# Row tiles 4 and 5 of layer 2 without quarter folding in the inverse transform along d, in a kernel of two GFNet and two squared-ReLU layers

## The chip, the cores and the metric

The kernel runs on one core of one Trainium2 chip. The metric is device time in microseconds of that core, lower is better; the time before is a median of three runs. A profiled execution also shows the engines' work: PE (TensorE, matrix multiply; its weight loads are shown as PEld), DVE (VectorE), ACT (ScalarE), POOL (GpSimd) and SP, which here only issues DMAs.

## The reference, cut to what matters

```
def _A_ref(x, w_r, w_i):                      # x: 1 x 2048 x 448, bfloat16
    X = rfft2(x.astype(float32), axes=(-2, -1))
    X = X * (w_r + 1j * w_i)                  # w: 2048 x 225
    return irfft2(X, s=(S, D)).astype(bfloat16)

def _B_ref(x, w1, b1, w2, b2):                # w1: 448 x 1792
    h = relu(x @ w1 + b1)
    return (h * h) @ w2 + b2

x = A_x
for layer in range(2):
    x = x + _A_ref(layernorm(x), A_w_r, A_w_i)
    x = x + _B_ref(layernorm(x), B_w1, B_b1, B_w2, B_b2)
```

Each of the two layers filters all 2048 rows together in the frequency domain (a transform along the rows, s, and one along the 448 columns, d), and then runs a feed-forward network (FFN) on each row by itself.

## The kernel before, in words

Everything between the input and the output stays on chip. The 2048 rows are 16 row tiles of 128 (row 16 p + t is in tile t, partition p). The transforms are matmuls with constant matrices. Per layer the stages are:

- forward transform, per row tile in part A (A1, A2), then per pair p of low row frequencies: along d (TD), along the remaining row digit (B), the product with the weights on DVE (W), and the inverse of that digit (Bi). Their results go through `VT`, and every row tile needs all pairs.
- inverse along d per group of row tiles, `stage_TI` (line 1087), and the last inverse digit with the residual addition, `stage_AI` (line 1109). Groups are tile 0, tile 1, then pairs (2, 3), (4, 5) up to (14, 15). The layer norm statistics of the FFN (`ln_B`, line 1164) follow per group: a sum of squares (lines 1170 and 1171, on ACT or DVE), a square root (line 700, ACT), a reciprocal, and the transposed row tile `yT`, by `flip` (line 1151: matmuls with a reversed identity and a copy out of PSUM) for tiles 0 and 1, and by a transposing DMA (line 668, on SP) for the others; tiles 4 to 15 are scaled first (lines 717 and 718).
- FFN in four chunks of four row tiles. Chunk 0 has two groups of first-layer matmuls, for tiles 0 and 1 and for tiles 2 and 3 (`h_part`, line 1266, widths of 256); chunks 1 to 3 pair half-height matmuls of width 512 (`h_pairs`, line 1226). ACT does the ReLU out of PSUM (line 700), DVE squares it (line 735). `o_tile` (line 1280) is the second matrix product of one tile, 14 matmuls, and its addition to the residual (line 1292). In layer 2 each row tile then goes to memory.

**The two ways through the inverse along d.** A transform matrix along 448 columns has mirror symmetry: the right half of the cosine part is the mirror image of the left half, that of the sine part too, with a sign. Both ways use this (half folding: only 224 columns come out of `stage_TI`). Quarter folding uses it once more, on even and odd frequencies apart. With `late` true, `stage_TI` makes four separate products of 112 columns per tile, `stage_AI` adds and subtracts them on DVE by four `tt` (line 735, two from `tmp` to `VT`, two back) and then needs two matmuls of 224 columns per tile. With `late` false, `stage_TI` sums pairs of matmuls of 224 columns in PSUM, there is no `tt`, and `stage_AI` has four matmuls of 448 columns for a group of two tiles. Either way `stage_TI` has eight matmuls for a group of two, `stage_AI` four, ACT copies 2 x 448 columns out of PSUM (line 706), and DVE has two residual additions (line 1146).

`late` is `t >= LATE[L]`: with `LATE = (4, 4)` tiles 4 to 15 of both layers are quarter folded.

**The order of the work.** The program first lists all operations, grouped into units (a PSUM tile's matmuls, or one operation of another engine). A unit's number is its place in that list. `ORDER` fixes, for each engine, the sequence of unit numbers. The class `_Sched` then gives out PSUM banks in that order, sets the semaphore waits, and, by its own model of the times, puts filler matmuls on a constant (line 1415) where it sees PE idle. For copies out of PSUM that both ACT and DVE can do (`evac`, lines 706 and 707), the engine whose list holds the unit does them. Engines run their lists strictly in order.

Units that the text uses, with the numbers of before: layer 1: TI of tile 1 is 287 and 289 with copies 288 and 290, of tile 0 270 and 272 with copies 271 and 273; copies of TI of tiles 4/5 319, 6/7 337, 10/11 375, 12/13 393 (matmuls 392), 2/3 305, 14/15 411; folding sums 320 to 323 (tiles 4/5), 376 and 377 (tiles 10/11); square roots of tiles 0 and 1 277 and 294; first FFN matmuls 428. Layer 2: copy of the last tile's A2 858; Bi 944 and 946 with copies 945 and 947; copy of Bi 953; TI of tile 0 961 and 963 with copies 962 and 964, of tile 1 978 and 980 with copies 979 and 981; flip of tile 0 969 with copy 970, of tile 1 986 with copy 987; square roots 968 and 985; copies of TI of tiles 2/3 996, 4/5 1011, 6/7 1029, 8/9 1049, 10/11 1067, 12/13 1085; tiles 4/5: TI 1010, the four `tt` 1012 to 1015, AI 1016, residual additions 1017 and 1018; scaling of tile 7 1042; squares of tiles 10/11 1075 and 1076; TI of tiles 14/15 1102; first FFN matmuls 1120.

Of the kernel before, what the change touches and what calls it, by code (L numbers as in the profile page):

```python
# [36 lines left out]
def make_constants():  # L37
# [76 lines left out]
ADJ = {}  # L114
ORDER = {
    "pe": """
# [10 lines left out]
1354""",  # L127
    "act": """
# [12 lines left out]
1315 1325 1323 1330 1328 1335 1333 1338 1340""",  # L141
    "dve": """
# [23 lines left out]
1331 1329 1101 1334 1336 1339 1341 1119 1346 1349 1343 1352 1355""",  # L166
    "pool": """
12 15 13 16 17 14 18 20 19 22 21 53 69 61 23 77 24 85 25 116 119 26 142 145 129 132 158 155""",
    "sp": """
3 6 4 8 10 28 30 29 36 32 40 41 39 31 27 34 45 37 33 47 46 38 44 35 314 269 334 352 354 355 372 390 408 426 1005 1026  # L170
1044 1046 1064 1082 1047 1100 1118 1250 1209 1306 1303 1203 1212 1253 1259 1300 1297 1350 1206 1347 1256 1344 1353
1356""",
}
STAY = 3000.0
LOOK = {}
# [3 lines left out]
A1GROUPS = ((0, 1), (1, 1), (2, 1), (3, 1), (4, 1), (5, 1), (6, 2), (8, 2), (10, 2), (12, 2), (14, 2))  # L179
ACT_STATS = (1, 3, 5)  # L180
HALVES = True
LATE = (4, 4)


class _Op:
# [395 lines left out]
def bass_interleave_layers__spectral_gfnet__dense_activation_squared_relu__prompt_kernel(nc, A_x, A_w_r, A_w_i, B_x, B_w1, B_b1, B_w2, B_b2, out):  # L581
# [6 lines left out]
    with ExitStack() as es:  # L588
# [758 lines left out]
        def ffn(last):  # L1347
# [4 lines left out]
            for t, n in TGROUPS:  # L1352
                base = PR["ramp"][L] - PR["rstep"][L] * t if t < 4 else PR["late"][L] - PR["lstep"][L] * t
                sch.bias, sch.tag = base + PR["TI"][L], f"TI{L}.{t}"
                stage_TI(t, n, t >= LATE[L])
                sch.bias, sch.tag = base + PR["AI"][L], f"AI{L}.{t}"
                stage_AI(t, n, not last, t >= LATE[L])
                sch.bias, sch.tag = base, f"ln{L}.{t}"
# [135 lines left out]
```

## Time and profile before

| what | value |
|---|---|
| median of 3 runs | 267.29 us (266.42 to 267.77) |
| profiled execution, its own time | 267.07 us |
| its span, first to last instruction | 265.1 us |
| busy PE, DVE, ACT | 257.7, 204.1, 172.8 us |
| layer 1: inverse along d begins, first FFN matmul | 42.7, 50.3 us |
| layer 2: inverse along d begins, first FFN matmul | 166.8, 173.0 us |

Times in the profile are us from the first instruction, and each instruction carries the line of the helper that made it: nearly all matmuls are L681, copies out of PSUM L706 on ACT and L707 on DVE, sums and products of two tensors L735. Matmuls are pipelined, so that the length of one holds its latency, and the pace of a row of them is read from several. A row of the timeline merges neighbours of one kind: start, length from the first start to the last end, engine, line, operation, output<-inputs, shape, count, and in brackets the idle time ahead of it with what ended it. `TIo`, what `stage_TI` leaves, and the quarter folded sums lie in the buffers `tmp` and `VT` and appear under these names; `W1_sb` and `W2_sb` both appear as `W_sb`.

### The profile page before, as it was taken

Reading aid. Unit: us, or ns where it says so; the run is one execution under the profiler, and the core shown is the slowest. Engines: PE = TensorE matmul, PEld = TensorE weight load, DVE = VectorE, ACT = ScalarE, POOL = GpSimd, SP = SyncE. Lnnn points to the kernel's source line nnn. Section 1 sums busy time; section 2 is a strip of 40 time slices with the busy share of each in tenths; the row PEclk is TensorE's granted clock in tenths of the full one; section 3 lists DMA queues with packets and bytes.
Section 4 is the critical chain, followed back from the end, with each engine's and each line's share of the span. In section 5 each row is a group of like instructions: output and inputs, shape, how many; then the busy total and the mean of one; then the engine's idle time right before and its main releaser. Section 6 shows DMA issues by size and latency. Waiting matters only on the chain.

```text
span 265.1 us, 5674 instructions
## 1 busy us (share of the span) xinstructions
PE 257.7 (97%) x2127; PEld 163.0 (61%) x2127; DVE 204.1 (77%) x658; ACT 172.8 (65%) x375; POOL 14.3 (5%) x32
## 2 busy tenths in 40 slices
PE   8999989999999999999999999999999999999996
PEld 2686768797544555665558756789654465554454
DVE  3878998999969983489998899899964069921662
ACT  5887897999449447893216889999634886121820
POOL 8840000000000000000000000000000000000000
PEclk9999999999999999999999999999999999999999
DMA  7999700032300224000000000022232000220053
GB/s 226 383 262 350 262 3 2 0 72 41 74 2 1 42 39 80 2 0 2 0 1 2 2 0 2 0 45 41 42 69 45 2 0 2 40 41 2 0 176 104
DMA packets 25531, 16.33 MB, mean 62 GB/s; under 512 B 18174, under 2 KB 24542, under 8 KB 25504
## 3 DMA queue, kind: packets, MB, share of 16 engines
q1 hardware_dynamic: 24768, 14.25, 20.5%
q10 hardware_dynamic: 576, 0.92, 1.0%
q0 software_dynamic: 160, 0.81, 0.8%
q8 instruction: 17, 0.28, 0.5%
q14 instruction: 10, 0.08, 0.1%
HBM read 10.46 MB, written 1.84 MB: 46 GB/s over the span
## 4 chain that ended last, share of the span: by engine, by line
PE 80%; DVE 9%; ACT 6%; DMA 3%; issue 1%; SPq 1%; DVEq 0%
PE ps L681 80%; DVE tmp L735 6%; DMA xin<-in_A_x_dram 3%; DVE arena L735 2%; ACT VT L706 2%; ACT tmp L706 2%; ACT arena L706 2%; SPq L673 1%; DVE st L825 0%; ACT yT L706 0%; ACT mv L700 0%; PE ps L1415 0%; ACT Fs L717 0%; DVE VT L707 0%; DVE x_sb L1292 0%
## 5 line engine op out<-in xcount | busy, mean ns | idle before, releaser
L681 PE MATMUL ps<-yT,W_sb 64*128 64x512 bf16 (+1 forms) x770 | 90.3, 346 | 0.1
L681 PE MATMUL ps<-W_sb,arena 128*128 128x448 bf16 (+3 forms) x476 | 87.0, 342 | 0.0
L681 PEld LDWEIGHTS ps<-yT,W_sb 64*128 64x128 bf16 (+1 forms) x770 | 54.5, 95 | 31.9 <-ACT arena L700 1.3
L700 ACT ACTIVATE arena<-ps,b1col 128x512 bf16<-128x512 f32 x84 | 51.9, 689 | 28.7 <-PE ps L681 28.6
L681 PEld LDWEIGHTS ps<-W_sb,arena 128*128 128x128 bf16 x476 | 45.4, 98 | 38.5 <-DVE arena L735 1.5
L735 DVE TENSOR_TENSOR arena<-arena 128x512 bf16<-128x512 bf16 (+1 forms) x140 | 45.5, 362 | 24.7 <-ACT arena L700 24.5
L706 ACT ACTIVATE arena<-ps 128x448 bf16<-128x448 f32 (+1 forms) x41 | 26.0, 705 | 4.8 <-PE ps L681 4.7
L1170 ACT ACTIVATE VT<-x_sb 128x448 bf16<-128x448 bf16 x28 | 16.1, 579 | 16.6 <-DVE x_sb L1146 16.6
L700 ACT ACTIVATE mv<-mv,epst 128x1 f32<-128x1 f32 (+1 forms) x45 | 12.5, 296 | 17.0 <-DVE mv L826 14.0
L700 ACT ACTIVATE arena<-ps 128x256 bf16<-128x256 f32 x56 | 18.0, 386 | 0.6 <-PE ps L681 0.5
L681 PE MATMUL ps<-arena,G_sb 128*128 128x448 bf16 (+1 forms) x84 | 16.9, 335 | 0.9 <-ACT arena L706 0.9
L1292 DVE SCALAR_TENSOR_TENSOR x_sb<-ps,mv,arena 128x448 bf16<-128x448 f32 (+2 forms) x13 | 8.3, 643 | 12.0 <-PE ps L681 11.9
L706 ACT ACTIVATE XA<-ps 128x512 bf16<-128x512 f32 x26 | 14.2, 591 | 4.7 <-PE ps L681 4.7
L681 PE MATMUL ps<-H_sb,arena 128*128 128x256 bf16 x128 | 15.8, 273 | 1.2 <-DVE arena L735 0.6
L706 ACT ACTIVATE VT<-ps 128x1024 bf16<-128x1024 f32 (+2 forms) x20 | 14.0, 772 | 3.0 <-PE ps L681 3.0
L681 PE MATMUL ps<-yT,VT 64*128 64x512 bf16 x42 | 15.8, 376 | 0.0
L735 DVE TENSOR_TENSOR tmp<-arena,Wt 128x896 bf16<-128x896 bf16 x26 | 15.3, 620 | 0.6 <-ACT arena L706 0.4
L681 PEld LDWEIGHTS ps<-H_sb,arena 128*128 128x128 bf16 x128 | 11.7, 98 | 5.0 <-DVE arena L735 3.4
L681 PE MATMUL ps<-TD_sb,XA 112*128 112x112 bf16 (+3 forms) x232 | 14.4, 230 | 0.3 <-ACT arena L706 0.2
L681 PEld LDWEIGHTS ps<-TD_sb,XA 112*128 112x128 bf16 (+3 forms) x232 | 12.3, 103 | 3.1 <-ACT arena L706 0.8
L706 ACT ACTIVATE tmp<-ps 128x896 bf16<-128x896 f32 (+1 forms) x16 | 12.7, 853 | 1.1 <-PE ps L681 1.0
L681 PEld LDWEIGHTS ps<-arena,G_sb 128*128 128x128 bf16 x84 | 7.7, 98 | 6.5 <-ACT arena L706 1.5
(84 smaller groups left out, 299.0 us busy)
## 6 DMA issues: line engine op xcount, KB each, us to landing
out_dram<-x_sb SPq DMA_DIRECT2D x15, 112.0 KB, 1.8
W_sb<-in_B_w_dram SPq DMA_DIRECT2D x1, 1568.0 KB, 12.9
W_sb<-in_B_w_dram SPq DMA_DIRECT2D x1, 1344.0 KB
xin<-in_A_x_dram ACTq DMA_DIRECT2D x4, 224.0 KB, 5.2
xin<-in_A_x_dram SPq DMA_DIRECT2D x4, 224.0 KB, 7.2
H_sb<-c_H SPq DMA_DIRECT2D x1, 896.0 KB, 8.2
G_sb<-c_G SPq DMA_DIRECT2D x1, 672.0 KB, 9.5
Wt<-in_A_w_i_dram SPq DMA_DIRECT2D x1, 393.8 KB, 5.5
```

The costliest lines, as they stand in the source:

```text
L673: return e.dma_start(o, i)
L681: return sch.add("pe", lambda e: e.matmul(_res(o), lhsT, rhs, start=start, stop=stop, skip_group_check=skip), [lhsT, rhs], [o], cost=cost, ...
L700: sch.add("act", lambda e: e.activation(o, _res(i), func, **kw), rd, [o], cost=c)
L706: op = sch.add(engs[0], lambda e: e.activation(o, _res(i), ACT.Copy) if h[0].eng == "act" else e.tensor_copy(o, _res(i)), [i], [o], cost=c ...
L735: sch.add(eng, lambda e: e.tensor_tensor(o, _res(a), b, op), [a, b], [o], cost=_free(o) / rate + 69.0)
L1170: op = sch.add("act", lambda e, i=i, o=o, x=x, h=h: e.activation(o, x, ACT.Square, accum_out=sd[:, i, 1:2]) if h[0].eng == "act" else e.sc ...
L1292: small(lambda e: e.scalar_tensor_tensor(out=o, in0=_res(i), scalar=rs[0] if rs else 1.0, in1=xi, op0=ALU.add if t >= 4 and last else ALU. ...
```

## The change

`LATE` becomes `(4, 6)`: tiles 4 and 5 of layer 2 take the way of tiles 0 to 3. Layer 1 computes as before. The four `tt` of that group (1012 to 1015) are gone, so every later unit's number is four lower: AI of tiles 4/5 is 1012, its residual additions 1013 and 1014, and so on. All the lists of `ORDER` but POOL's are new, for both layers. In the part below, the lists are cut to the stretches around the two ramps and SP's list; among the moves between engines are, in layer 1, copies 260 and 288 from DVE to ACT and 283 from ACT to DVE; in layer 2, copies 858, 866, 869, 953, 962, 970 and 987 from DVE to ACT and 863, 871, 979 and 981 from ACT to DVE.

```diff
--- before.py
+++ after.py
@@ -114,62 +114,61 @@
 ADJ = {}
 ORDER = {
     "pe": """
...
-304 274 410 295 356 306 278 324 299 282 428 455 446 437 380 449 464 440 443 452 458 398 342 461 503 467 491 497 506
...
-839 742 837 807 860 822 864 757 857 865 861 882 868 870 880 878 884 902 896 894 914 904 900 930 898 918 916 920 932
-942 940 946 944 938 954 950 952 948 956 958 978 961 980 963 1084 982 965 1028 995 969 1066 986 1048 997 973 1010 990
-1120 1144 1147 1153 1138 1102 1132 1141 1016 1135 1150 1129 1034 1156 1198 1192 1177 1189 1168 1186 1054 1171 1162
...
+410 295 336 356 278 306 299 324 282 428 392 455 449 446 452 380 437 440 461 464 443 458 342 479 485 497 500 476 398
...
+843 807 727 860 822 742 757 857 864 861 865 882 870 868 878 880 884 902 896 894 918 904 898 900 914 920 916 930 940
+932 942 944 946 938 948 952 950 954 956 958 961 978 1080 963 980 1044 965 1024 995 982 1010 969 997 986 1062 1012 1098
+973 990 1116 1140 1143 1125 1149 1030 1134 1131 1152 1128 1137 1146 1050 1068 1161 1167 1158 1170 1185 1182 1191 1188
...
     "act": """
...
-258 268 375 319 337 393 305 411 294 277 296 279 300 283 357 310 309 431 311 429 328 438 447 450 456 435 327 441 453
...
-871 881 879 885 903 897 895 905 901 915 899 919 917 931 921 943 941 933 945 947 939 955 951 949 959 979 981 1085 1029
-996 985 968 1067 1049 1011 1000 1001 1002 1121 1145 1148 1127 1125 1123 1103 1142 1154 1139 1133 1136 1020 1019 1021
-1151 1157 1130 1023 1190 1169 1037 1193 1178 1172 1038 1199 1196 1163 1057 1166 1187 1039 1160 1181 1042 1175 1184
...
+258 268 288 375 319 305 411 294 296 277 357 279 300 310 309 337 311 433 429 393 450 456 453 447 431 435 328 327 329
...
+869 879 881 885 903 897 895 919 905 899 901 915 921 917 931 941 933 943 945 947 939 949 953 951 955 959 962 1081 1045
+1025 996 968 1011 970 985 987 1063 1000 1099 1001 1002 1121 1123 1141 1144 1015 1126 1016 1117 1017 1150 1135 1119
+1129 1132 1153 1019 1138 1147 1171 1162 1159 1183 1034 1186 1192 1189 1165 1168 1033 1035 1038 1071 1072 1054 1174
+1053 1195 1177 1073 1156 1180 1055 1090 1076 1215 1217 1212 1210 1222 1225 1220 1230 1232 1227 1259 1257 1262 1264
...
     "dve": """
...
-260 266 288 290 273 376 292 271 293 320 321 275 377 276 322 323 297 280 298 281 308 307 379 326 339 378 394 325 312
...
-888 877 889 876 887 890 891 909 907 893 908 892 906 911 910 924 922 912 913 923 925 927 926 928 929 934 935 936 937
-953 957 962 964 983 966 984 967 970 1030 971 988 972 987 989 974 998 960 991 999 1031 1012 1013 1050 1003 1004 1033
-1051 1014 1053 1015 1032 1052 1126 1146 1018 1122 1017 1155 1140 1036 1008 1069 1022 1124 1035 1024 1137 1025 1007
...
+246 266 290 271 273 292 293 320 275 321 276 322 297 323 298 280 308 281 307 283 326 325 377 376 312 313 378 379 338
...
+877 886 876 889 887 890 891 906 892 893 908 909 907 910 911 925 923 912 913 922 924 926 927 928 929 934 935 936 937
+957 979 964 981 966 1082 967 1026 983 1027 971 984 998 972 988 999 989 1083 960 974 991 1046 1013 1029 1028 1047 1003
+1004 1014 1064 1084 1049 1032 1031 1065 1018 1048 1066 1067 1020 1145 1052 1133 1021 1051 1122 1151 1142 1139 1006
...
     "sp": """
-3 6 4 8 10 28 30 29 36 32 40 41 39 31 27 34 45 37 33 47 46 38 44 35 314 269 334 352 354 355 372 390 408 426 1005 1026
-1044 1046 1064 1082 1047 1100 1118 1250 1209 1306 1303 1203 1212 1253 1259 1300 1297 1350 1206 1347 1256 1344 1353
-1356""",
+3 6 4 8 10 28 30 29 36 32 40 41 39 31 27 34 45 37 33 44 38 47 35 46 314 334 352 354 355 372 390 269 408 426 1005 1022
+1040 1042 1060 1205 1208 1078 1043 1202 1096 1114 1255 1302 1296 1246 1249 1293 1252 1299 1199 1346 1340 1343 1349
+1352""",
 }
...
 HALVES = True
-LATE = (4, 4)
+LATE = (4, 6)
```

More of the change, by code (lines that the diff above doesn't have):

```diff
@@ L116 @@
     "pe": """
[10 rows of a table removed]
-1354""",
[9 rows of a table added]
+1234 1239 1104 1300 1297 1291 1247 1253 1294 1244 1250 1303 1308 1313 1318 1323 1328 1333 1341 1344 1338 1347 1350""",
     "act": """
 5 7 11 2 9 72 56 66 57 50 58 73 100 88 74 82 103 89 106 90 113 63 93 139 79 87 126 71 108 152 118 147 121 131 134 157
[11 rows of a table removed]
-1315 1325 1323 1330 1328 1335 1333 1338 1340""",
[11 rows of a table added]
+1314 1316 1319 1321 1324 1326 1331 1329 1334 1336""",
     "dve": """
 0 64 1 65 48 98 49 96 68 52 59 99 51 97 75 80 60 102 67 81 109 76 111 83 84 101 112 110 135 137 92 115 91 136 138 124
[22 rows of a table removed]
-1331 1329 1101 1334 1336 1339 1341 1119 1346 1349 1343 1352 1355""",
[22 rows of a table added]
+1330 1335 1337 1345 1339 1342 1348 1351""",
     "pool": """
```

60 rows, old and new, of the table ORDER are left out of this document.

## The prediction

> **What bounds the kernel now.** I read the page first: the profiled execution spans 265.1 us and counts as 267.07 us, so 2.0 us lie around the span; the median of the three runs, 267.29 us, stands 0.22 us above it.
>
> ```profile
> span 265.1 us, 5674 instructions
> PE 257.7 (97%) x2127; PEld 163.0 (61%) x2127; DVE 204.1 (77%) x658; ACT 172.8 (65%) x375; POOL 14.3 (5%) x32
> ```
>
> PE (the matmul engine) is busy nearly all the time, but a share over the span does not say what ends a stage. So I next read the windows by stage, cut where layer 2's inverse transform along d begins (166.8) and where its first FFN matmuls begin (173.0). Columns: length, then busy time and instruction count of PE, PEld, DVE, ACT and POOL, the granted clock, DMA.
>
> ```profile
> 166.80:173.00 6.20, 6.08 (x77) 5.11 (x78) 5.19 (x18) 5.60 (x11) 0.00 (x0) 1.00 0.00 0
> 173.00:180.00 7.00, 7.00 (x73) 6.18 (x71) 6.95 (x24) 6.91 (x22) 0.00 (x0) 1.00 0.21 43
> 180.00:190.00 10.00, 10.00 (x84) 7.98 (x82) 10.00 (x38) 9.67 (x33) 0.00 (x0) 1.00 0.14 28
> 173.00:198.00 25.00, 25.00 (x198) 18.41 (x196) 22.79 (x82) 18.66 (x59) 0.00 (x0) 1.00 0.27 52
> 198.00:254.00 56.00, 56.00 (x425) 28.11 (x423) 29.83 (x77) 29.21 (x53) 0.00 (x0) 1.00 0.11 24
> ```
>
> From 173 to 254 PE has no gap at all: whatever matmul time is added or taken there moves the end one for one. Between 173 and 190 DVE and ACT are full as well, so three engines are at their limit there. Third, the chain that ended last, around this place (start, length, what):
>
> ```profile
> 162.40 4.33 ACT VT L706 x6
> ...
> 166.87 3.48 PE ps L681 x41
> ...
> 170.35 0.91 ACT tmp L706
> 171.26 0.36 ACT mv L700 x2
> 171.62 0.82 ACT tmp L706
> ...
> 172.48 47.63 PE ps L681 x403
> ```
>
> The **ramp** from 166.8 to 173 is a latency chain through ACT: copies of the d-transform (L706 to tmp), then the two square roots of tiles 0 and 1 (L700), then PE takes over and keeps the chain.
>
> **The change part by part.** *Matmuls.* For tiles 4 and 5 together both ways issue eight matmuls in stage_TI and four in stage_AI; only their widths double. Unfolded, the eight are 224 wide instead of 112, the four 448 wide instead of 224. Prices from the timeline (start, length, instructions merged):
>
> ```profile
> 170.28 0.56 PE L681 MATMUL ps<-TI_sb,VT 112*128 112x112 bf16 x8
> 168.16 0.94 PE L681 MATMUL ps<-tmp,FI_sb 128*128 128x224 bf16 x8
> 177.78 0.55 PE L681 MATMUL ps<-tmp,FI_sb 128*128 128x224 bf16 x4
> 171.31 0.93 PE L681 MATMUL ps<-tmp,FI_sb 128*128 128x448 bf16 x4
> ```
>
> Eight of width 112 take 0.56 us and eight of width 224 take 0.94 us (the row is of another stage, with the same moving width): +0.38. Four of width 224 take 0.55 and four of width 448 take 0.93: +0.38. **PE gets +0.76 us.** The granted clock is 1.00 in every window above, so nothing has to be added for it.
> One page speaks for less. The Trainium skill, TensorE: Matmul & The Clock Gate, section Back-to-back issue gap, says that in a stream of weight load and matmul pairs the spacing is set by both and gives about 81 ns at 128 columns; by that, widening 112 to 224 (whose streaming takes 93 ns at its 2.4 GHz) would cost about 0.1 us for the eight, an estimate, and the whole sum would fall by about 0.3 us. This trace disagrees: eight matmuls of width 112 would need 0.65 us at 81 ns each, and they took 0.56 with the last one's whole latency in it.
>
> *VectorE.* The four tensor_tensor of the folding go (half of the pair sums, half of the output sums), each on 128x448.
>
> ```profile
> 174.28 1.28 DVE L735 TENSOR_TENSOR VT<-tmp 128x448 bf16<-128x448 bf16 x4
> ```
>
> Four in a row take 1.28 us, so **DVE loses 1.3 us**. I count it as 0 on the end: PE waits for nothing between 173 and 198 (25.00 of 25.00 above). Bounds: 0, and -1.3 if DVE set the pace there (a rival below). The copy of the transform (128x896) and the residual additions keep their sizes: 0.
>
> *The new order, layer 2's ramp.* All five lists are rewritten, so every move counts as the change's. Before the second square root (unit 968 in the old list, 985 in the new) ACT has the copies 979, 981, 1085, 1029, 996. In the new list it has 962, 1081, 1045, 1025, 996, 1011 and the flip copy 970: one half copy less, the copies of tiles 8/9 and 4/5 more, and a flip copy that DVE did before.
>
> ```profile
> 167.39 0.74 ACT L706 ACTIVATE tmp<-ps 128x224 bf16<-128x224 f32 x2
> 169.53 1.73 ACT L706 ACTIVATE tmp<-ps 128x896 bf16<-128x896 f32 x2 [0.26 <-PE ps L681]
> 171.03 0.55 DVE L707 CAST yT<-ps 128x384 bf16<-128x384 f32 x1
> 48.92 1.58 ACT L706 ACTIVATE yT<-ps 128x384 bf16<-128x384 f32 x4
> ```
>
> That is -0.37 + 2 x 0.87 + 0.5 = +1.9 us of ACT ahead of that root; ACT was idle 6.20 - 5.60 = 0.60 us of the window, which absorbs some. Following PE, ACT and DVE through the new lists with these durations, I get the first FFN matmul at 174.4 instead of 172.95, +1.45 us (bounds: +1.3, the ACT work less all the idle; +1.9, none absorbed). But PE no longer idles through it: the new list has TI of tiles 14/15 (1098, old 1102) and AI of tiles 4/5 (1012, old 1016) ahead of the FFN. Those are 0.56 and 0.55 us by the rows above, some 0.38 each at the pace of a stream, so 0.76 us of old work leaves the full stretch behind. Net of the ramp: +1.45 - 0.76 = **+0.7 us, with the 0.76 of new work inside**; the slack of the ramp neither grows nor shrinks. Bounds +0.5 and +1.1.
>
> *Ahead of the ramp.* The old order lets ACT wait for the copy 945, while PE does 946 first; the new PE list has 944 first. Against that, ACT gets the copy 953 from DVE.
>
> ```profile
> 162.40 4.91 ACT L706 ACTIVATE VT<-ps 128x1024 bf16<-128x1024 f32 x8 [0.40 <-PE ps L681]
> ```
>
> The idle 0.40 ahead of this row goes, one copy comes (eight take 4.91; the small ones among them are some 0.5): +0.1. I set it off against an earlier start of layer 2's W stage, where the copy 858 of the last row tile moves to ACT, beside DVE: 0, bounds -0.4 to +0.5.
>
> *Layer 1's ramp.* ACT's new list takes the copies 337 and 393 out from ahead of the two roots and puts in the half copy 288.
>
> ```profile
> 42.70:50.30 7.60, 7.28 (x89) 6.00 (x90) 7.00 (x23) 6.97 (x14) 0.00 (x0) 1.00 0.01 2
> 43.74 4.96 ACT L706 ACTIVATE tmp<-ps 128x896 bf16<-128x896 f32 x6 [0.51 <-PE ps L681]
> 48.55 0.52 ACT L700 ACTIVATE mv<-mv,epst 128x1 f32<-128x1 f32 x2
> 47.95 0.62 DVE L1171 SCALAR_TENSOR_TENSOR VT<-x_sb 128x448 bf16<-128x448 bf16 x1
> 50.26 0.49 PE L681 MATMUL ps<-yT,W_sb 128*128 128x256 bf16 x3
> ```
>
> Six copies in 4.96 are 0.83 each: -1.66 + 0.37 = -1.3 on ACT. But DVE's sum of squares for tile 0 (47.95 to 48.57) is nearly as late as the root, and DVE's list ahead of it is only one half copy and two folding sums shorter, about 1.0 us, part of it spent waiting for matmuls anyway. I take the FFN's start 0.5 us earlier, and 0.38 of it comes back, since TI of tiles 12/13 (unit 392) now follows the first FFN unit: **-0.1**, bounds -0.9 to +0.3. The forward stages of layer 1 are a nearly full DVE chain with the same work in both lists; the reordering there I take as 0, within 0.4 either way, by the 0.40 of the row of 162.40, the largest wait quoted for such a stage.
>
> *Queues.* SP now issues the outputs of tiles 2 and 3 ahead of the transposes of tiles 10/11, and that of tile 1 ahead of those of 12/13.
>
> ```profile
> 195.00 7.52 SPq L668 DMA_TRANSPOSE yT<-arena  x2
> 187.17 10.76 PE L681 MATMUL ps<-W_sb,arena 128*128 128x448 bf16 x56
> 201.49 1.67 PE L681 MATMUL ps<-yT,W_sb 64*128 64x512 bf16 x13
> ```
>
> The transpose of tiles 10/11 ended its issue at 202.52. It now waits for tile 3's output sum, right after the 56 matmuls that end at 197.93, and for two issues. What reads it, FFN chunk 2, comes behind 78 half-height matmuls that start near 198.2; at 1.51 us per 14 (one of the two forms is merged into its neighbour's row) those end near 206.7. The cover is about 4 us: 0. Without it, each us late would be a us. The TQ load moves behind the transposes of tiles 10/11 of layer 1, and is first read in the second forward transform tens of us later: 0. The filler matmuls are set anew in PE's idle time: 0.
>
> **Sum**: +0.7 (of which 0.76 is the matmuls) + 0 - 0.1 = +0.6 us on 267.07, 267.7; with the 0.22 by which the median stands above the profiled execution, **267.9 us**, +0.2% of 267.29.
>
> **The rivals.** *ACT becomes the bound after 173 (slower).* In the old order the last copy of the FFN's second group ends before the third tile's output needs it:
>
> ```profile
> 188.36 0.64 ACT L700 ACTIVATE arena<-ps 128x256 bf16<-128x256 f32 x2
> 193.24 0.58 ACT L1170 ACTIVATE VT<-x_sb 128x448 bf16<-128x448 bf16 x1 [3.30 <-DVE x_sb L1146]
> ```
>
> The copies end at 189.0; tile 2's output starts two quarters into the row of 187.17, at 192.5: cover 3.5 us, and ACT then idles 3.30. In the new ACT list the squares 1071 and 1072 of tiles 10/11 and the scaling 1038 of tile 7 stand before the last copies, and 1038 waits for a DVE reciprocal that stands far back in DVE's list. With ACT starting 1.45 late and two squares (0.58 each) more, against copies done earlier, I put the last copy at 190.5 with no wait and near 192.6 with the waits that I can follow, against a need at 193.4. If ACT or DVE run over 0.8 us later than that, PE waits, us for us. A typical overrun of one of ACT's stalls, 1 to 2 us beyond the point, gives 268.9 to 269.9; I take 269.3. For it: ACT 6.91 of 7.00 and 9.67 of 10.00. Against: the cover is there on paper.
> *DVE sets the pace in 173 to 190 (faster).* DVE is at 10.00 of 10.00. If PE's full windows hide a wait for DVE in each instruction, 1.3 us less DVE pays, and the matmuls fall into the room: 267.9 - 0.76 - 1.3 = 265.8. Against: no idle on PE or its weight loads is put down to DVE there.
> By the Trainium skill, Perfetto Trace Analysis, section Identifying the Most-Contended Engine, occupancy is a fair measure for VectorE and a bad one for matmul, which would speak for this rival.
> *The first ramp gives all it can (about the same or faster).* -0.9 in place of -0.1: 267.1.
>
> **How the numbers follow.** About 0.5%, or 1.34 us, is what a measurement of this kernel can tell from no change: the borders are 265.95 and 268.63. My sum with the rival of the first ramp: 0.57, of which 0.02 falls below and 0.03 above the borders by the unpriced reordering; ACT as the bound: 0.31, of which 0.28 lies above 268.63; DVE as the pace: 0.12, of which 0.10 lies below. So faster 0.12, same 0.57, slower 0.31. Low end of the range: the sum with the best of both ramps and of the stages ahead, 267.9 - 0.8 - 0.2 - 0.4 = 266.5, drawn down to 266.2 for part of the DVE case. High end: the ACT rival's upper end, 269.9.
>
> **What would show it.** Right: PE 25 of 25 us behind the ramp, the FFN's start in layer 2 about 1.4 us later against what precedes it, the L735 groups with VT and tmp at 22 instead of 24 instructions each, and layer 1's first FFN matmul up to 0.5 us earlier. Wrong: idle time of PE put down to ACT or DVE near 188 to 194 (ACT the bound), a full PE with a lower start-to-end time from 173 to 254 than 0.76 less (DVE the pace), or a first ramp off by over 0.9 us.

## The result, and the profile after

The changed kernel takes 267.31 us (median of 20 runs, 267.03 to 267.87); the kernel before, beside it, took 266.44 us (median of 20 runs, 266.20 to 267.77). The ratio is 1.0021, 95% interval 1.0011 to 1.0031: a small slowdown, +0.56 us by the ratio. (The two medians stand 0.87 us apart; the ratio is not their quotient.) The forecast was +0.6 us, to 267.9, and "the same" as the likeliest answer. The change of time held roughly; that answer did not, and neither did the base: it came from three runs whose median lay 0.85 us above the median of the twenty.

The page of the kernel after, first the same two lines:

```profile
span 265.3 us, 5657 instructions
PE 257.6 (97%) x2127; PEld 167.9 (63%) x2127; DVE 202.1 (76%) x653; ACT 173.2 (65%) x376; POOL 14.2 (5%) x32
```

The number of matmuls is the same, DVE has 2.0 us less work, and PE is as busy as before. The windows by stage (length, then busy time and instruction count of PE, PEld, DVE, ACT and POOL, granted clock, DMA); the first is the ramp of layer 2, from its first matmul of the inverse along d to its first FFN matmul, the last the ramp of layer 1:

```profile
166.40:173.93 7.53, 7.38 (x89) 6.29 (x89) 6.43 (x21) 7.21 (x14) 0.00 (x0) 1.00 0.00 0
173.00:180.00 7.00, 7.00 (x70) 6.11 (x69) 6.96 (x23) 6.91 (x23) 0.00 (x0) 1.00 0.21 42
180.00:190.00 10.00, 10.00 (x87) 8.22 (x85) 9.99 (x37) 8.30 (x28) 0.00 (x0) 1.00 0.16 31
173.00:198.00 25.00, 25.00 (x196) 18.47 (x195) 24.37 (x85) 18.11 (x60) 0.00 (x0) 1.00 0.26 52
198.00:254.00 56.00, 56.00 (x423) 31.16 (x422) 26.86 (x70) 28.84 (x51) 0.00 (x0) 1.00 0.15 40
42.10:49.40 7.30, 6.76 (x81) 5.51 (x82) 6.46 (x20) 6.73 (x14) 0.00 (x0) 1.00 0.01 2
```

PE is full from 173 to 254 as before, and DVE, despite its smaller load, is still at 9.99 of 10.00 from 180 to 190: the order brings other work forward into the room. The chain that ended last has lost its ACT links in layer 2's ramp:

```profile
163.72 2.64 PE ps L680 x22
166.36 0.02 issue
166.38 0.39 ACT VT L705
166.78 0.05 issue
166.82 96.20 PE ps L680 x751
```

From 166.82 to 263.02 the chain is PE's matmuls alone. Before, it ran through ACT's copies and square roots until 172.48. So what an order could win in that ramp by feeding PE is taken, and every matmul column that is added shows.

The first matmuls of the inverse along d, the widened ones of tiles 4 and 5 (the two rows in the middle), and the first FFN matmuls, in the timeline of the kernel after:

```profile
166.43 1.78 PE L680 MATMUL ps<-TI_sb,VT 112*128 112x224 bf16 x19
170.23 0.93 PE L680 MATMUL ps<-TI_sb,VT 112*128 112x224 bf16 x8
172.58 0.92 PE L680 MATMUL ps<-tmp,FI_sb 128*128 128x448 bf16 x4
173.93 0.94 PE L680 MATMUL ps<-yT,W_sb 128*128 128x256 bf16 x7
```

The widened ones took 0.93 and 0.92 us where the folded ones took 0.56 and 0.55.

**Where the time went.** Engines run their lists in order, so the start of one and the same matmul can be compared in two traces. The traces begin differently: the last row tiles' first transform began at 16.34 us before and at 15.87 us after.

```profile
16.34 0.27 PE L681 MATMUL ps<-Fs,xin 128*128 128x256 bf16 x1
```

```profile
15.87 0.27 PE L680 MATMUL ps<-Fs,xin 128*128 128x256 bf16 x1
```

In 11 of the 12 experiments below it began 0.5 to 0.9 us earlier than in the profile of before, and only new_second_half was as late, so the profile of before is one that began late. Differences below are therefore counted from this point. After less before: last matmuls of the last output tile (their start 261.89 before, 262.16 after) +0.27 + 0.47 = **+0.74 us**. The same difference ("by the trace" below) is given for each experiment, beside its ratio; it has no scatter of the start in it, but is one execution.

### The profile page after: what moved, and what is told of

It is laid out like the page before. It is cut to its first block, busy times and chain, and to the rows that moved or that the text cites. A ratio compares the mean times of both kernels' runs of the same rounds, so it can differ in the third digit from the quotient of the medians.

```text
span 265.3 us, 5657 instructions
## 1 busy us (share of the span) xinstructions
PE 257.6 (97%) x2127; PEld 167.9 (63%) x2127; DVE 202.1 (76%) x653; ACT 173.2 (65%) x376; POOL 14.2 (5%) x32
## 3 DMA queue, kind: packets, MB, share of 16 engines
HBM read 10.46 MB, written 1.84 MB: 46 GB/s over the span
## 5 line engine op out<-in xcount | busy, mean ns | idle before, releaser
L680 PEld LDWEIGHTS ps<-yT,W_sb 64*128 64x128 bf16 (+1 forms) x770 | 58.2, 95 | 27.6 <-ACT arena L699 1.2
L734 DVE TENSOR_TENSOR arena<-arena 128x512 bf16<-128x512 bf16 (+1 forms) x140 | 44.8, 365 | 31.3 <-ACT arena L699 31.1
L705 ACT ACTIVATE arena<-ps 128x448 bf16<-128x448 f32 (+1 forms) x40 | 25.4, 714 | 5.7 <-PE ps L680 5.4
L705 ACT ACTIVATE XA<-ps 128x512 bf16<-128x512 f32 (+1 forms) x27 | 14.5, 585 | 8.0 <-PE ps L680 8.0
L705 ACT ACTIVATE VT<-ps 128x1024 bf16<-128x1024 f32 (+2 forms) x22 | 15.3, 754 | 1.5 <-PE ps L680 1.4
```

Of the source, the lines that this page charges most:

```text
L680: return sch.add("pe", lambda e: e.matmul(_res(o), lhsT, rhs, start=start, stop=stop, skip_group_check=skip), [lhsT, rhs], [o], cost=cost, ...
L705: op = sch.add(engs[0], lambda e: e.activation(o, _res(i), ACT.Copy) if h[0].eng == "act" else e.tensor_copy(o, _res(i)), [i], [o], cost=c ...
L734: sch.add(eng, lambda e: e.tensor_tensor(o, _res(a), b, op), [a, b], [o], cost=_free(o) / rate + 69.0)
```

## The experiments

Two theories had been left by the prediction: **PE sets the pace** behind the ramp (theory 1: the price is the width of the matmuls, and what DVE saves is worth nothing) and **DVE sets the pace from 173 to 190** (theory 3). Theory 2 was that the price is in the new order. Each kernel was timed beside the kernel before, whose medians lay between 266.46 and 266.78 us.

**1. The computation without the new order, and the order in halves.** Three kernels share their parts: the old lists with the four `tt` struck, and the new lists up to about 100 us or from there on.

```diff
 # old_order_unfolded: the lists of before without 1012 to 1015, later units renumbered
-LATE = (4, 4)
+LATE = (4, 6)
 # new_second_half: the same, and the new lists from layer 2's transforms on
 # new_first_half: LATE = (4, 4), the new lists for layer 1 only
```

> The old lists of before, with tiles 4 and 5 of layer 2 unfolded: the four folding sums are struck from VectorE's list, nothing else moves. Theory 1, the doubled widths pay where PE has no idle time: +0.7 to +0.8 us on before (ratio 1.0028). Theory 2, the slowdown comes from the new lists: no more than +0.2 us (ratio 1.000 to 1.001). Theory 3, VectorE sets the pace behind the ramp, so that its four sums fewer pay: -0.5 us or faster (ratio below 0.998).

> Old lists for what starts before 100 us, new lists behind that, tiles 4 and 5 of layer 2 unfolded. Theory 1: the whole slowdown is in here, +0.6 us on before (ratio 1.002), since the new ramp of layer 2 neither saves nor loses beside the wider matmuls. Theory 2: also slower, by as much as the change, so this run tells only the halves apart; if the first ramp's new order costs or saves, this run differs from the change by that, at most 0.3 us by the traces.

> New lists for what starts before 100 us, old lists behind that, all quarter folding kept as before. Theory 1: the first half's order is about neutral, -0.2 to +0.2 us on before (ratio 0.999 to 1.001). Theory 2: if the new lists are what costs, part of it is here, +0.3 us or more (ratio 1.001 or above).

Measured: old order, unfolded: 267.61 us, ratio 1.0033 (1.0015 to 1.0051), by the trace +1.03. New second half: 267.29 us, 1.0015 (0.9998 to 1.0033), +0.80. New first half: 266.74 us, 1.0004 (0.9986 to 1.0023), +0.19. So the slowdown needs no new order: the unfolding brings it in the old one too. The new first half on its own changes nothing that can be measured; its first FFN matmuls come 0.46 us earlier and 0.40 of that is given back by the second FFN chunk, as work that stood ahead of them now stands behind.

In the old order the trace shows the price in three steps: +0.37 at the ramp, where the eight wider matmuls stand, +0.38 at the four wider ones of `stage_AI`, and a wait:

```profile
180.77 2.79 PE L681 MATMUL ps<-yT,W_sb 128*128 128x256 bf16 x24 [0.16 <-DMA yT<-x_sb]
```

The matmuls that wait are the first FFN ones of tiles 2 and 3, and what they wait for is the transposing DMA of these tiles. Against the pace of the stream the gap is 0.32 us. This wait is the 0.3 us by which the old order is dearer than the new one by the traces.

**2. The matmuls alone.** Before, with the twelve matmuls of tiles 4 and 5 issued four times.

```diff
-    mm(q[...], v, TI_sb[:, r, g, 0:QD], True, True)
+    for again in range(4 if sch.tag == "TI1.4" else 1):
+        mm(q[...], v, TI_sb[:, r, g, 0:QD], True, True)
...
-    for i in range(n):
+    for i in [i for i in range(n) for again in range(4 if sch.tag == "AI1.4" else 1)]:
```

> Before, with the twelve folded matmuls of tiles 4 and 5 in layer 2 each issued four times instead of once, into the same places; VectorE's folding sums stay. It computes the same products again and again. That is three times the columns that the change adds, so 3 x 0.76 = 2.3 us more for PE. Theory 1: +2.1 to +2.5 us on before (ratio 1.008 to 1.009). Theory 2 or 3, PE has room or waits hide it: clearly less, under 1.2 us (ratio below 1.0045).

Measured: 268.83 us, ratio 1.0071 (1.0042 to 1.0101), by the trace +2.28: 3 x 0.76 us, of it 1.17 at the ramp and 1.11 behind. (The ratio's middle is below the 1.008 that was expected; its interval reaches past it.)

```profile
171.96 1.75 PE L681 MATMUL ps<-TI_sb,VT 112*128 112x112 bf16 x32
178.39 1.70 PE L681 MATMUL ps<-tmp,FI_sb 128*128 128x224 bf16 x16
```

Less the latency of the last one (0.21 and 0.26 us for a single one), 32 matmuls of width 112 go at 50 ns each and 16 of width 224 at 96 ns. PE's time is added one for one, also in the ramp, where PE idled for 0.12 us of the 6.20.

**3. All tiles unfolded, and two more folded.** The size changed in both directions, in old lists.

```diff
-LATE = (4, 4)
+LATE = (4, 16)   # all_unfolded_layer_2: all 24 sums of layer 2 struck
+LATE = (4, 2)    # fold_2_3_too: tiles 2 and 3 get four sums
```

> The old lists, with all six groups from tile 4 on unfolded in layer 2: 24 folding sums are struck from VectorE's list. PE gets 6 x 0.76 = 4.6 us, VectorE loses 24 x 0.3 = 7 us. Theory 1: +3.8 to +4.6 us on before (ratio 1.014 to 1.017), the lower end if the ramp's idle 0.8 us takes part of it. Theory 3: less than +1 us or faster.

> The same step the other way: tiles 2 and 3 of layer 2 are quarter folded too, in the old lists, with their four new sums, the matmuls behind them, their residual additions and statistics set in a little later. PE loses 0.76 us, VectorE gets 1.2. Theory 1: -0.76 us if every cover holds (ratio 0.997), nothing left if the later transpose of tiles 2 and 3 makes the second group of FFN matmuls wait by 0.7 us or more. Theory 3: slower by up to 1.2 us (ratio up to 1.0045).

Measured: all unfolded: 270.82 us, ratio 1.0157 (1.0137 to 1.0176), +4.2 by the trace. Folding tiles 2 and 3 too: 269.62 us, 1.011 (1.0093 to 1.0127), +3.1. Windows from 173 to 198, all unfolded first, then tiles 2 and 3 folded too:

```profile
173.00:198.00 25.00, 24.94 (x189) 18.09 (x188) 17.24 (x62) 19.28 (x59) 0.00 (x0) 1.00 0.25 47
```

```profile
173.00:198.00 25.00, 23.71 (x183) 16.77 (x182) 23.02 (x82) 18.50 (x58) 0.00 (x0) 1.00 0.21 43
```

With everything unfolded DVE falls from 22.79 to 17.24 us in these 25 us, and the kernel loses most of the widening's 6 x 0.76 = 4.6 us: DVE's time is worth nothing there. The second kernel is a miss. It takes 0.76 us from PE and loses 3.1 us. The ramp is not where it loses: counted from the common point, its first FFN matmul comes 0.14 us earlier than in the kernel before. Behind that PE is idle 1.3 us of these 25, and filler matmuls (0.2 us each) that the kernel before does not have here stand in its list, two in the ramp and four between 178 and 189 us. The waits from 166 to 192 us are for ReLU copies (L700) and residual additions (L1146), which free PSUM banks, and for the layer norm (L735):

```profile
PEld ps L681 <- ACT arena L700: 1.5, 4, 0.8
PEld ps L681 <- DVE x_sb L1146: 1.5, 2, 1.1
PE ps L681 <- DVE x_sb L1146: 1.1, 2, 0.9
PEld ps L681 <- DVE x_sb L735: 0.8, 1, 0.8
```

So this kernel tests the lists and the fillers made for it more than the folding, and the size of its loss is not explained piece by piece. Neither more nor less folding in these lists beats the kernel before; whether lists made for folding tiles 2 and 3 would, wasn't tried.

**4. DVE's time alone, more of it.** The four sums of one pair of tiles issued twice, the second time over the same result.

```diff
+    def tt_(o, a, b, op):
+        u = sch.new_unit("dve")
+        for again in range(2 if sch.tag == "AI1.4" else 1):   # sums_10_11_twice: "AI1.10"
+            sch.add("dve", lambda e: e.tensor_tensor(o, a, b, op), [a, b], [o], ..., unit=u)
```

> Before, with each of the four folding sums of tiles 4 and 5 in layer 2 issued twice in a row; the result is the same. VectorE gets 1.2 to 1.3 us more, as much as the change takes from it, in a stretch where it is full. Theory 1, VectorE's queue has room against PE behind the ramp: 0 to +0.3 us on before (ratio 1.000 to 1.001). Theory 3, VectorE sets the pace there: +1.0 to +1.3 us (ratio 1.004 to 1.005).

> Before, with the four folding sums of tiles 10 and 11 in layer 2 each issued twice: the same 1.2 to 1.3 us more of DVE's time in the stretch in which it is full as with tiles 4 and 5's sums twice, but with about 1.4 us of other PE work between the sums and the matmuls that read them. Theory 1 (PE sets the pace, and a sum costs only where a matmul waits for it): 0 to +0.2 us, ratio 1.000 to 1.001. Theory 3 (DVE sets the pace from 173 to 190 us): +1.0 to +1.3 us, ratio 1.004 to 1.005.

Measured: tiles 4 and 5: 267.70 us, ratio 1.0039 (1.0025 to 1.0054), +1.25 by the trace. Tiles 10 and 11: 267.78 us, 1.0043 (1.0028 to 1.0058), +1.31. Both are misses for theory 1 as it stood, and at first sight theory 3's number. The waits say where it comes from. Tiles 4 and 5 twice, waits from 173 to 182 (engine, tile and line, what for, total us, times, longest):

```profile
PEld ps L681 <- DVE tmp L1126: 1.4, 2, 0.9
PE ps L681 <- DVE tmp L1126: 0.9, 2, 0.8
```

Tiles 10 and 11 twice, the timeline around the one gap of PE:

```profile
184.88 1.12 DVE L1126 TENSOR_TENSOR tmp<-VT 128x448 bf16<-128x448 bf16 x3
185.92 0.28 DVE L735 TENSOR_TENSOR arena<-arena 128x256 bf16<-128x256 bf16 x1
186.12 0.68 DVE L1151 SCALAR_TENSOR_TENSOR x_sb<-ps,mv,x_sb 128x448 bf16<-128x448 f32 x1
186.95 0.54 PE L681 MATMUL ps<-tmp,FI_sb 128*128 128x224 bf16 x4 [1.05 <-DVE x_sb L1151]
```

In the first the doubled sums are what the very next matmuls read. In the second the matmuls wait for something else: the residual addition of tile 8, queued behind the doubled sums on DVE, which frees the PSUM bank that they write. In the kernel before, the same addition ends at 185.71 and its reader starts at 186.35:

```profile
185.04 0.67 DVE L1146 SCALAR_TENSOR_TENSOR x_sb<-ps,mv,x_sb 128x448 bf16<-128x448 f32 x1
186.35 0.55 PE L681 MATMUL ps<-tmp,FI_sb 128*128 128x224 bf16 x4
```

In the second kernel 0.15 us lie between the addition's end (186.80) and the matmul, so of the 0.64 some 0.5 us is cover. The doubled sums move the addition by 1.7 us against the rest (186.12 + 0.62, by which this trace is earlier up to there, less 185.04; each of the four repeated sums is issued 0.42 us behind the one whose result it writes over), and 1.7 - 0.5 = 1.2 us is the gap of 1.22 that the stream shows. I had looked for cover at the sums' own matmuls and overlooked what stands behind them in DVE's queue.

**5. DVE's time alone, less of it.** Adding can't tell an engine that sets the pace from one that runs half a microsecond ahead of it; taking away can.

```diff
+        k = slice(0, 1 if sch.tag == "AI1.4" else None)
+        sch.add("dve", lambda e: e.tensor_tensor(o[..., k], a[..., k], b[..., k], op), [a, b], [o], ...)
```

> Before, with the four folding sums of tiles 4 and 5 in layer 2 cut to four elements a partition each (so these tiles are not folded, and their matmuls run as before on unfolded data): what DVE saves of the change, about 0.9 us in its full stretch, without the 0.76 us of wider matmuls. Theory 1 (PE has no room, DVE stands up to 0.5 us ahead of it): 0, within 0.15 us, ratio 0.9995 to 1.0005. Theory 3 (DVE sets the pace from 173 to 190 us): -0.7 to -0.9 us, ratio 0.997.

Measured: 266.72 us, ratio 1.0004 (0.9993 to 1.0016). Theory 3's 0.997 is outside. Windows of this kernel:

```profile
173.00:180.00 7.00, 6.92 (x69) 5.97 (x66) 6.20 (x24) 6.91 (x22) 0.00 (x0) 1.00 0.23 43
180.00:190.00 10.00, 9.78 (x80) 7.78 (x81) 9.75 (x37) 9.13 (x31) 0.00 (x0) 1.00 0.16 31
```

DVE has room now, and the end does not move up. By the trace this execution was even 0.49 us longer than before, all of it at one gap of 0.47 us:

```profile
180.22 2.03 PE L681 MATMUL ps<-yT,W_sb 128*128 128x256 bf16 x17 [0.30 <-DMA yT<-x_sb]
```

It is the wait of experiment 1 again, in a kernel whose matmuls are those of before. The two views of this transposing DMA (median us from issue to landing, the kernel before first):

```profile
yT<-x_sb SPq DMA_TRANSPOSE x1, 3.1
```

```profile
yT<-x_sb SPq DMA_TRANSPOSE x1, 4.7
```

Issued at 175.49, it landed at 175.49 + 4.7 = 180.19, when PE had been ready for 0.47 us. The ratio's upper end, 1.0016, is 0.43 us, and its middle 0.1 us, so the wait is unlikely to be in all of this kernel's runs. Nor does the wait hide a gain: both kernels have the same matmuls in the same order, and matmul by matmul, counted from the common point, this one stands 0.01 us behind the kernel before from 161 to 179.4 us and 0.49 us behind from 180.6 us to the end. On neither side of the gap has DVE's saved time moved a matmul forward.

**6. Filling the wait.** In the old order a unit of PE is moved ahead of the matmuls that waited for the transposes.

```diff
 # PE, old_order_filled: AI of tiles 8 and 9 (1050) ahead of the FFN matmuls of tiles 2 and 3
-1152 1194 1188 1173 1185 1164 1182 1050 1167
+1152 1050 1194 1188 1173 1185 1164 1182 1167
 # DVE, filled_sums_early: besides, the residual additions 1052 and 1051 right behind it
-1031 1020 1133 1021 1007 1187 1064 1052 1067 1066 1124 1051
+1052 1031 1051 1020 1133 1021 1007 1187 1064 1067 1066 1124
```

> Same as the kernel with the old order and unfolded tiles 4 and 5, but one unit of PE (the inverse along the second axis for tiles 8 and 9) stands ahead of the first layer-2 FFN unit that reads tiles 2 and 3's transposes, to fill the 0.32 us that PE waited there. Theory 1 (PE is full, the price is the width of the matmuls, and the rest of the old order's 1.0 us was that wait): 0.3 us less than with the old order as it was, +0.7 to +0.8 us on before, ratio 1.0028. Rival (the wait is only where the time shows, and something behind it holds PE back anyway): unchanged, ratio 1.0033, with the wait again at a later unit.

> As the filled old order, but DVE takes the two sums of tiles 8 and 9 that free the PSUM banks of the moved unit right behind it, 3 us sooner, instead of where the old list has them. If the filled order lost its gain because PE and ACT ran out of PSUM banks, the wait of 0.32 us at the transposes is gone and nothing takes its place: +0.7 to +0.8 us on before, ratio 1.0028. Rival (ACT's copies hold PE back whatever the banks): +1.0 to +1.5 us, ratio 1.004 to 1.005.

Measured: filled: 268.19 us, ratio 1.0053 (1.0039 to 1.0066), +1.84 by the trace: worse than either expectation. With the sums early: 267.46 us, 1.0030 (1.0019 to 1.0042), +0.99. In the first the wait for the transposes is gone, and PE waits for ACT instead. The second row is the next `stage_AI` unit, with its wait; the first is a filler matmul (0.2 us at the pace of a stream) that has come in ahead of it besides:

```profile
186.74 0.38 PE L1415 MATMUL ps<-ones 128*128 128x512 bf16 x1
187.51 0.56 PE L681 MATMUL ps<-tmp,FI_sb 128*128 128x224 bf16 x4 [0.39 <-ACT arena L700]
```

Taking the sums early removes that gap, which is in line with PSUM banks as its cause: the moved unit had held its banks from 180.3 until DVE had read them at 185.8, and now gives them back at 183.3. It isn't a clean proof, since the filler matmul went as well. And two small waits remain, for ACT's and DVE's release of banks, 0.09 and 0.19 us against the pace, in place of the 0.32 at the transposes:

```profile
181.27 1.21 PEld L681 LDWEIGHTS ps<-yT,W_sb 128*128 128x128 bf16 x12 [0.20 <-ACT arena L700]
182.78 0.77 PEld L681 LDWEIGHTS ps<-yT,W_sb 128*128 128x128 bf16 x8 [0.31 <-DVE x_sb L1146]
```

By the trace only 0.04 us is won on the unfilled order, by the ratios no difference can be told. The expectation of +0.7 to +0.8 is within the ratio's interval and not in the trace; I count it as not settled.

**7. The wait of ACT ahead of the ramp.** The prediction gave the new order some gain for putting Bi's matmuls 944 ahead of 946. Here the two change places in the kernel before, and nothing else.

```diff
 # PE
-942 940 946 944 938
+942 940 944 946 938
```

> Before, with two neighbours of PE's list exchanged, the Bi units 944 and 946, so that ScalarE finds its next copy ready; nothing else changes. The row at 162.40 shows ScalarE idle 0.40 us there, on the chain. If that idle is on the path to the ramp: -0.2 to -0.4 us (ratio 0.9985 to 0.9993); if the last Bi pair, which waits for VectorE, ends the stage anyway: 0 (ratio 1.000).

Measured: 266.50 us, ratio 0.9991 (0.9978 to 1.0004), +0.01 by the trace: 0, the second of the two expectations. Without that idle time ACT is not earlier at the ramp:

```profile
161.31 4.47 ACT L706 ACTIVATE VT<-ps 128x1024 bf16<-128x1024 f32 x6
166.09 0.66 ACT L706 ACTIVATE VT<-ps 128x256 bf16<-128x256 f32 x2 [0.32 <-PE ps L681]
```

It waits for PE a few copies later instead. The first matmul of the inverse along d comes 0.16 us earlier by the trace, and the matmuls at 167.7 us are as late as before.

## Why the prediction was right or wrong

**The step that failed is the last one, from the sum to the answer.** The mechanism was right: the wider matmuls are paid on a full PE, DVE's saving is worth nothing, and the sum of +0.6 us is a slowdown of 0.2%. But the prediction took 0.5%, or 1.34 us, as the least that a measurement can tell from no change, gave "the same" a chance of 0.57, and gave "slower" 0.31, nearly all of it for ACT as the bound. No run had measured that border; the three runs at hand lay 1.35 us apart. With 20 runs of each kernel the ratio is 1.0021 with an interval of 1.0011 to 1.0031, 0.1% to either side: the kernel is slower, by the cause that the sum names and not by the rival to which "slower" was given. Two terms were mis-sized besides, layer 1's ramp and the base. Part by part:

- **Matmuls, +0.76, right.** The rows of the kernel after give 0.93 - 0.56 + 0.92 - 0.55 = 0.74 us, and the kernel with the matmuls four times shows 2.28 = 3 x 0.76. The Trainium skill, TensorE: Matmul & The Clock Gate, section Back-to-back issue gap, had about 81 ns for a pair of weight load and matmul at 128 columns; the trace does not agree, with 50 ns at width 112.
- **VectorE at 0, right, and shown.** Cutting the four sums short (from 173 to 190 DVE's busy time falls from 16.95 to 15.95 us) left the time where it was. By the Trainium skill, Perfetto Trace Analysis, section Identifying the Most-Contended Engine, occupancy would have pointed to DVE at 10.00 of 10.00; here it did not set the pace. The reason given, that PE waits for nothing there, was the right one. What it did not say is how small DVE's lead is: some 0.5 us at tile 8's addition.
- **Layer 2's ramp, right.** From the first matmul of the inverse along d (166.87 before, 166.43 after) to the first FFN matmul (172.95, 173.93) it took 1.42 us longer, forecast 1.45. The old work that now stands ahead of it then comes off: counted from the common point, the first FFN matmul is +1.45 us late, the first of the second chunk +0.61, the last output tile +0.74.
- **Ahead of the ramp at 0, right as a sum, wrong in a part.** The ramp begins 0.44 us earlier than in the profile of before (166.87 to 166.43), where the common point is 0.47 us earlier, so 0.0. But the 0.40 us of ACT's idle time that "goes" is worth nothing by itself: in experiment 7 it turned into another wait.
- **Layer 1's ramp at -0.1, mis-sized.** The first FFN matmul comes 0.90 us earlier (50.26 to 49.36), the ramp's first matmul 0.61 earlier (42.74 to 42.13), so the ramp gives 0.29, not 0.5; 0.39 is given back, forecast 0.38. The ramp itself costs 0.1 instead of saving 0.1. The reordered forward stages, taken as 0, gave 0.14, so that at the second FFN chunk layer 1 has come out at about 0.
- **ACT as the bound after 173, no.** PE's weight loads wait for ACT 0.5 us in all from 166 to 198 in the kernel after, in two pieces, and its matmuls are not among the waits; ACT falls from 9.67 to 8.30 of 10.00. Waits like those that this rival feared are seen in experiment 6, in an order that holds PSUM banks longer.
- **Queues at 0, right as far as it goes.** PE is full from 198 to 254 past the transposes and outputs that moved. That the transposes of tiles 2 and 3 need up to 4.9 us instead of 3.1 was not in the reckoning: the profile of before shows the short case. The kernel after has the short case too.
- **The sum, +0.6, was measured as +0.56 by the ratio, +0.74 by the trace and +0.87 by the medians.** With layer 1 at 0 it would have been +0.7, near what the trace shows. More mis-sized was the base: I added 0.22 us to come from the profiled execution (267.07) to a median of three (267.29). That execution began 0.5 us later than nearly all others, and the median of twenty is 266.44. Taken from there, the same sum gives 267.0, and 267.31 was measured. So 267.9 came out only 0.6 us high because a change that was taken too small made up for part of a base that was 0.85 us too high.

The whole says: the change takes 1.3 us from DVE, which runs beside a full PE, and pays with 0.76 us on PE. By one trace each the new order (+0.74) is 0.3 us better than the old one with the same computation (+1.03), and the difference is the wait for the transposes of tiles 2 and 3. By the ratios (1.0021 and 1.0033, with intervals that overlap) the two orders can't be told apart, and whether that wait is in most runs of the old order stays open.

## What to carry to other kernels

Where several engines are full, ask which one never waits: here work taken from DVE was worth nothing, and columns added to PE were paid almost in full. To find out whether a full engine sets the pace, take work away from it; adding work also costs where it merely stands half a microsecond ahead, through whatever is queued behind it on its engine, PSUM releases above all. And take the base from many runs: here a median of three runs lay 0.85 us off, as much as the whole effect. How small a change can be told is itself read from the scatter of many runs; it decides whether a right sum is called "the same" or "slower".

## What the runs showed of the hardware that was not expected

- The start of a program differs between executions: the last row tiles' first matmuls came at 16.34 us in the profile of before, and 0.5 to 0.9 us earlier in 12 of the 13 others, most of which have the same lists up to there. Why was not looked into.
- One transposing DMA, that of tiles 2 and 3, landed 3.0 to 3.1 us after its issue in nine of the 14 profiled executions and 4.6 to 4.9 us in the five others (old_order_unfolded, folding_sums_twice, old_order_filled, sums_struck, filled_sums_early). The DMA packets in the traces show what goes with it. In the five, a packet of the queue that the page of the profile names `q8 instruction` begins 0.86 to 0.94 us after the DMA's first packet, and the DMA's packets start over 2.5 to 2.9 us; in the nine none begins in the first 1.2 us, and the packets start within 1.4 to 1.5 us. Of the 181 transposing DMAs in the 14 traces nine took 4 us or more. Each of these has a packet of an instruction queue (`q8` or `q14`) that begins between 0.05 us before its first packet and 0.94 us after; of the 172 others one has, and it took 3.5 us. So a collision with the loading of instructions is the likely cause; no experiment moved that loading, so it is not shown. In the four kernels whose work up to there in layer 2 is that of before (before, bi_order_mended, sums_10_11_twice, new_first_half) the packet comes 1.28 to 1.57 us after the first one, which speaks for the program, and not chance, as what decides.
- A DVE sum that writes over the result of the one ahead of it was issued 0.41 to 0.43 us after it (folding_sums_twice, sums_10_11_twice), where independent ones followed at 0.30.
